# A fused adaLN block: first V as the first matrix work, K and Q weights loaded as halves, softmax denominators as a column of V

## The chip, the core and the metric

The kernel runs on one core of a Trainium2 chip. The metric is the device time of one execution in microseconds (us); lower is better. The core has five engines with a queue each that runs in order: PE (matrix multiply into PSUM, with its weight loads shown as PEld), DVE (vector), ACT (scalar functions, table driven), POOL (general) and SP, which here only issues DMA transfers. They wait for each other through semaphores alone.

## The reference, cut to what matters

S = 2048 tokens, D = 448, H = 16 heads of Dh = 28, F = 1792, all in bf16. Six modulation vectors come from a conditioning row, then follow attention over 8 positions with a stride of 2, and an MLP.

```
mod = silu(c) @ w_mod                      # sa, ca, ga, sb, cb, gb
h = layernorm(x) * (1 + ca) + sa
q, k, v = split(h @ wqkv)                  # 16 heads of 28
# position s attends to s, s-2, ..., s-14
attn = softmax(mask(q . k[s - 2w]) * Dh ** -0.5)
x = x + ga * (sum_w attn * v[s - 2w]) @ wo
h = layernorm(x) * (1 + cb) + sb
x = x + gb * (gelu(layernorm(h) @ w1 + b1) @ w2 + b2)
```

## The kernel before, in words

**Tiles.** Tokens lie as pairs: even and odd tokens are two independent sequences (`NS = 2`) of 1024, so that a stride of 2 becomes a stride of 1. Token tiles `p` = 0 to 7 hold 128 positions of both. A tile goes through layer norm (`front_ln`: statistics L455 and L457 on DVE, the power -0.5 at L466 or L468 on ACT or POOL, normalize L477 on DVE, 64 columns doubled by `tail`, L487 to L491), is transposed, and is scaled and shifted into `hT` (`affine`, L501 on DVE or L503 on ACT). Tiles 0 and 1 are transposed by PE (L534), tiles 2 to 7 by DMA (`zT`, L526).

**D = 448 on 128 rows.** The contraction has three full row tiles and a remainder of 64 rows. The remainder is kept twice, in rows 0 to 63 and 64 to 127, so that two remainder matmuls run side by side (`summed`: L547 full, L553 remainder; L561 is the first, piecewise form of L547).

**Q and K.** For tiles 0 and 1 the weights are first copied into groups of 32 columns per head (`spread`, L438 to L441, and `spread r`, L446 to L449), and Q and K come out transposed (`front_qk`, evacuated at L608). For tiles 2 to 7 (`natural_qk`) the raw weights are the moving operand, ACT or DVE brings the result to SBUF (`zy`, L627, L628), and a DMA transposes it into `qT` or `kT` (L630).

**Attention** runs in 9 batches of 114 positions. V of a batch is 16 matmuls (L705, batches 0 to 4) or 8 matmuls on windows copied by L688 (batches 5 to 8), evacuated into `vb` (L720 on ACT, L723 on DVE). `vb` has 32 columns per head, of which 28 hold V and 4 are zero. Logits `lt` (L737) go through exp on ACT (L744, two halves) and a mask product on DVE (L750). Then PE forms the denominators, `pd` (L759: ones times the masked exponentials, 8 matmuls of 464 columns), and the products `po` (L770, 64 rows in the trace). The denominator is inverted on ACT as exp(-ln): L779 reads `pd` from PSUM, L781 follows. DVE multiplies `po` by it into `qT` (`omul`, L787). After that come the output projection `pw` (L802), the second norm, and the MLP (`p` at L547, L553 and L882, gelu at L863).

**Phases.** Batches 0 to 4 come before the first MLP tile, batches 5 and 6 before the second, 7 and 8 before the last two; between them ACT changes its function table (L924, L931).

**Order.** Nothing is scheduled by rule at run time. `add` records tasks with the engines that could run them, and two tables of numbers, `ORDER` (the sequence in which tasks are recorded, with `:A`, `:D`, `:P`, `:R` for a task put on ACT, DVE, POOL or in its second form on PE, and `+n@m` for n dummy matmuls ahead) and `SLOTS` (the buffer of each short-lived tile), give the order on every queue. PSUM has four such slots (`P`, two banks each), shared by all matmul outputs.

**Loads.** All large loads are issued by SP in one queue: `load_x` L338, modulation weights L345 and L348, `load_qk` L324 (three row tiles of K and Q together), `load_rest` L328 (the 64 remainder rows, twice), `load_wv` L332 and L334. The dummy matmuls (`filler`, L381) multiply zeros.

Of the kernel before, what the change touches and what calls it, by code (L numbers as in the profile page):

```python
# [9 lines left out]
FP32 = mybir.dt.float32  # L10
# [39 lines left out]
]  # L50
ORDER = """
3 14 17 0 1 15 5 9 10 18 11 16 13 19 20 2 6 24 21 73 55+12@55 26 12 71 25 56 72 74 57 75 22 58 77 23 59 62 60 27 61 76
4 32 67 66 78 68+11@68 108 63 28 110 64 30 84:A 89:P 69 79 65 31 70 88:P 109 111 80 83 112:P 34 81 87:A 85 29 93:P
90:A 101+9@101 114 113 36 82 94+3@94 91 95 115:D 92:A 102 86 103 116 144 96 120:A 97 99 135 104 106 117:A 98 142 118:A
105 145 119:A 143 133 146 100 121 136 134 148 137 126 107 147 7 149:D 138 127 150 122 139 124 129 198 190 123 140 191
200 141 199 128 269 125 271 236 270 130 207 40 209 33 201 241 210 38 237 208 272 238 273 37 185 242 152 202 35 154 151
153:A 8 278 187 239 203 159 211 204 188 205:D 212 206 155 279 213 186 243 240 214:A 160 156 192 215 307 157 189 275
161 274 158 280 171 308 281 282 193 162 172 244 245 284 195 283 163 217 173 285 246 276:D 219 39 218 167 216 277 247
447 164 196 248 225 286 168 224 165 169:D 174 312 42 309 313 228 166 310 314 220 170 226 311 290 221 289 229 222 288
315 194 287 230 558 232 197 317 176 560 233 318 175 316 177 223 249 319 234 49 227 320 250 231 251 559 321 235 345 253  # L60
342 346 373:R 254 252 324 46 255 343 322 44 257 48 340 561 323 325 256 41 326 258 374 51 482 54 378 344 375 52 379 299
347 47 259 376 43 328 292 327 300 341 260 348 291 329 301 261 330 295 293 262 263 380 350 264 294 131 296 132 304 333
297 303 377 45 351 334 331 381 265 349 332 305 266 335 382 352 267:A 483 383 268 337 336 384 448 338:D 339 385 353 53
# [3 lines left out]
455 369 434 371 490 372 456 403 443 491 488 435 444 404:D 457 405 458 459 493 492 436 494 460 437 495 461 594 517 438  # L67
462 496 497 463 536 498 499 595 525 500 537 596:D 524 538 539 466 464 501 502 467 465 518 503 528 468 526 527 470 505
529 504 506 531 469 519 507 530 521 471 520 510 472 523 540 522 543 475 508 553 532 541 476 473 533 474 509 542 511
535 562 565 534 477 551 557 512 513 552 563 514 478 515:D 566 479 564 600 480 597 567 554 544 598 481 601 568 445 569  # L70
570 602 547 555 571 599 556 548 572 516 603 604 605 545 606 573 628 607 546 574 608 635 609 549 610 550 636 611 439
575 630 640 576 612 629 637 577 639 613 578 614 638 579 641 581 633 580 634 582 632 583 631 586 647 584 585 587 616
588 615 648 617 642 656 645 618 644 621 649 589 658 622 619 646 620 643 623 650 664 625 590 624 591 651 626:D 592 654
662 653 627 665 655 657 652 663 659 674 660 666 667 669 661 675 668 676 678 677 679 686 672 673 670 687 681 671 690
680 691 688 689 694 693 701 683 692 682 684 695 685 702 697 703 704 709 698 696 710 699 705 711 700 706 712 707 708
# [77 lines left out]
def kernel(  # L153
# [74 lines left out]
    ones_k = cst.tile([128, 2, HP], BF16, name="ones_k")  # L228
# [62 lines left out]
    def consts():  # L291
        for vb in vbufs:
            nc.vector.memset(vb[:, :, :, DH:HP], 0.0)
        nc.vector.memset(ones_k[:], 1.0)
        nc.vector.memset(ones_k[0:WIN - 1, 1, :], 0.0)

    dconst(0.45, consts, ["vpad", "ones"])
# [92 lines left out]
    add("PE", 0.45, c_cols, mode="32x128", reads=["c", "c1", "one1", "warm_w"], bufs=[psc], fills=[psc], name="c_cols")  # L390
    add("ACT", 0.12, lambda: nc.scalar.activation(out=e_c[:], in_=psc.t[:, 0, 0:128 * KT:128], func=ACT.Exp, scale=-1.0), bufs=[psc],
# [117 lines left out]
    def front_ln(u, on_act, dma=False):  # L509
# [452 lines left out]
```

## Time and profile before

| | |
|---|---|
| median of 3 runs | 170.06 us (169.41 to 172.02) |
| the profiled execution | 170.37 us |
| its span in the trace | 168.6 us, so 1.8 us lie around it |
| PE busy | 160.9 us |
| DVE busy | 113.2 us |
| ACT busy | 101.3 us |
| POOL busy | 42.0 us |
| granted TensorE clock | 1.0 |

The rows of the trace name line, engine, operation and tiles (out<-in), a count (x), and times in us or, for one instruction, in ns. A busy time counts an instruction from its start to its end as the profiler sees it. Instructions of one engine overlap a little there, so the pitch from start to start is often shorter than the duration.

### The profile page before, as it was taken

The numbers are of one execution on the slowest core, as the hardware profiler recorded it, in microseconds if no ns is written. First come the engines' busy times: TensorE is split into PE (matmuls) and PEld (weight loads), VectorE is DVE, ScalarE is ACT, GpSimd is POOL, SyncE is SP. The second block draws the span as 40 slices with busy tenths as digits, with TensorE's granted clock in tenths as the row PEclk, the third lists the DMA queues.
The fourth block names the chain that finished last, engine by engine and source line by source line (L and its number), as shares of the span: only waits on it lengthen the run. The fifth ranks groups of instructions, "written<-read, shape, count | busy, mean of one in ns | idle before, by whom it ended". The sixth has DMA issues, their size and how long they took to land.

```text
span 168.6 us, 4965 instructions
## 1 busy us (share of the span) xinstructions
PE 160.9 (95%) x2126; PEld 84.0 (50%) x2126; DVE 113.2 (67%) x277; ACT 101.3 (60%) x139; POOL 42.0 (25%) x69
## 2 busy tenths in 40 slices
PE   7999969987999999999999999999999999999992
PEld 4778535444554544435565443555544455344562
DVE  7869898758899969897837869465596940400112
ACT  3378888949379946869557167986318440099000
POOL 3235251002030400319300033850003156008100
PEclk9999999999999999999999999999999999999999
DMA  5999989699999799300150000028020006110002
GB/s 158 323 336 291 167 253 172 129 158 255 188 227 287 211 160 201 100 0 0 25 106 2 4 0 2 4 49 188 4 95 14 0 4 120 46 67 0 0 27 82
DMA packets 35573, 18.78 MB, mean 111 GB/s; under 512 B 28507, under 2 KB 34592, under 8 KB 35552
## 3 DMA queue, kind: packets, MB, share of 16 engines
q1 hardware_dynamic: 35548, 18.47, 47.6%
q8 instruction: 16, 0.26, 0.6%
q14 instruction: 5, 0.04, 0.1%
q10 hardware_dynamic: 4, 0.00, 0.0%
HBM read 9.81 MB, written 1.84 MB: 69 GB/s over the span
## 4 chain that ended last, share of the span: by engine, by line
PE 77%; DMA 13%; DVE 4%; issue 2%; POOL 2%; SPq 1%; ACT 1%; POOLq 0%; DVEq 0%
PE p L882 26%; PE p L547 22%; PE pw L802 7%; DMA zT<-zy 7%; PE pq L547 5%; PE p L553 4%; DMA x_all<-in_A_x_dram 4%; PE pv L547 3%; PE po L770 3%; DMA wm_st<-in_w_mod_dram 3%; PE lt L737 2%; DVE hT L501 2%; PE pv L705 2%; PE pd L759 1%; DVE stt L455 1%
## 5 line engine op out<-in xcount | busy, mean ns | idle before, releaser
L863 ACT ACTIVATE hm<-p,b_col 128x512 bf16<-128x512 f32 x56 | 33.6, 695 | 30.6 <-PE p L553 26.1
L882 PE MATMUL p<-w_s,hm 128*128 128x448 bf16 (+1 forms) x238 | 44.5, 342 | 0.0
L547 PE MATMUL p<-yT,w_s 128*128 128x512 bf16 x168 | 38.1, 380 | 0.0
L468 POOL TENSOR_TENSOR rs_all<-mvs,neg_half 128x2 f32<-128x2 f32 x23 | 16.4, 719 | 75.1 <-DVE mvs L457 75.1
L882 PEld LDWEIGHTS <-hm 128*128 128x128 bf16 x238 | 22.6, 98 | 18.9 <-issue 0.6
L547 PEld LDWEIGHTS <-w_s 128*128 128x128 bf16 x168 | 15.8, 98 | 21.0 <-issue 3.2
L888 DVE TENSOR_TENSOR x_all<-p,x1p 128x896 bf16<-128x896 f32 (+2 forms) x10 | 8.8, 899 | 23.7 <-PE p L882 23.7
L744 ACT ACTIVATE et<-lt 128x928 bf16<-128x928 f32 x18 | 16.1, 940 | 6.7 <-PE lt L737 6.6
L455 DVE BATCH_NORM_STATS2 stt<-x_all 128x6 f32<-128x448 bf16 x32 | 18.6, 610 | 1.6 <-DMA x_all<-in_A_x_dram 1.4
L547 PE MATMUL pq<-wqk_st,hT 128*128 128x448 bf16 x72 | 15.0, 353 | 1.8 <-DVE hT L501 1.5
L840 POOL TENSOR_TENSOR x1p<-x_all,gbb_bc 128x448 f32<-128x448 bf16 x16 | 16.5, 1060 | 0.0
L787 DVE TENSOR_TENSOR qT<-po,den 128x912 bf16<-128x912 f32 x9 | 10.0, 1106 | 7.1 <-ACT den L781 6.7
L802 PE MATMUL pw<-wo_s,qT 128*128 128x448 bf16 x64 | 13.1, 353 | 0.0
L750 DVE TENSOR_TENSOR et<-et,mask 128x928 bf16<-128x928 bf16 x18 | 11.0, 640 | 2.2 <-ACT et L744 2.1
L627 ACT CAST zy<-pq 128x896 bf16<-128x896 f32 x11 | 9.7, 911 | 2.7 <-issue 2.0
L809 DVE TENSOR_TENSOR x_all<-pw,x_all 128x896 bf16<-128x896 f32 x8 | 8.7, 1088 | 3.9 <-PE pw L802 3.9
L779 ACT ACTIVATE den<-pd 128x928 f32<-128x928 f32 x9 | 8.5, 952 | 4.7 <-PE pd L759 4.7
L818 DVE TENSOR_TENSOR h<-h,mod_bc 128x896 bf16<-128x896 bf16 x16 | 10.4, 655 | 0.2
L547 PEld LDWEIGHTS <-hT 128*128 128x128 bf16 x72 | 6.5, 98 | 8.1 <-DVE hT L501 2.0
L455 DVE BATCH_NORM_STATS2 stt<-h 128x6 f32<-128x448 bf16 x16 | 9.5, 611 | 0.1
L781 ACT ACTIVATE den<-den,den_bias 128x928 f32<-128x928 f32 x9 | 9.4, 1068 | 0.2
L802 PEld LDWEIGHTS <-qT 128*128 128x128 bf16 x64 | 6.0, 98 | 6.0 <-issue 0.4
(114 smaller groups left out, 177.3 us busy)
## 6 DMA issues: line engine op xcount, KB each, us to landing
w_s<-in_B_w_dram SPq DMA_DIRECT2D x7, 224.0 KB, 3.3
out_dram<-x_all SPq DMA_DIRECT2D x7, 224.0 KB, 2.0
x_all<-in_A_x_dram SPq DMA_DIRECT2D x3, 448.0 KB, 6.5
wmod<-in_w_mod_dram SPq DMA_DIRECT2D x3, 448.0 KB
w_s<-in_B_w_dram SPq DMA_DIRECT2D x3, 448.0 KB, 4.8
wqk_st<-in_A_wqkv_dram SPq DMA_DIRECT2D x3, 225.0 KB, 4.3
wm_st<-in_w_mod_dram SPq DMA_DIRECT2D x1, 672.0 KB, 4.6
x_all<-in_A_x_dram SPq DMA_DIRECT2D x2, 224.0 KB
```

The costliest lines, as they stand in the source:

```text
L455: add("DVE", 0.53, lambda: nc.vector.bn_stats(out=stt[:, w, b, 0:6], in_=src()), reads=reads, bufs=bufs, after=early if w == b == 0 else ( ...
L468: ways = {"POOL": (0.55 + 0.17 * n, lambda: nc.gpsimd.tensor_tensor(out=r, in0=v, in1=neg_half[:, 0:n], op=ALU.pow))}
L547: nc.tensor.matmul(out(), lhsT=lhs(kt, slice(0, 128)), rhs=rhs(kt, slice(0, 128)), start=first and kt == 0, stop=not first and kt == KT - 2)
L627: add("ACT", 0.80, lambda to=to, src=src: nc.scalar.copy(out=to(), in_=src()), bufs=[pq, st], reads=["zpad"], writes=[(st, 0)], name="evac ...
L744: exps.append(add("ACT", 0.83, lambda half=half, lt=lt: nc.scalar.activation(out=et.t[:, 2 * half:2 * half + 2].rearrange("p r m c -> p r ...
L750: nc.vector.tensor_tensor(out=ev, in0=ev, in1=mask[:], op=ALU.mult)
L787: nc.vector.tensor_tensor(out=qT[:, :, LEAD + q00:LEAD + q00 + 2 * WQ], in0=po.t[:, :, 0:NS * 4 * WQ].rearrange("p j (m c) -> p m j c", c=WQ),
L802: nc.tensor.matmul(pw.t[:, s, 0:D], lhsT=qT[:, KT * s + ft, LEAD + 128 * p:LEAD + 128 * p + 128], rhs=wo_s[:, ft, :], start=(ft == 0), sto ...
L818: add("DVE", 0.55, lambda vec=vec, op=op: nc.vector.tensor_tensor(out=h2.t[:], in0=h2.t[:], in1=vec.unsqueeze(1).to_broadcast([128, NS, D] ...
L840: add("POOL", 1.0, lambda n=n: nc.gpsimd.tensor_tensor(out=x1p.t[:, n, :], in0=xn(p, n), in1=gbb2_bc[:], op=ALU.add), reads=[f"x{p}", "gbb ...
L863: gelus.append(add("ACT", 0.585, lambda f=f, a=a, p1=p1s[g]: nc.scalar.activation(out=hm.t[:, f].rearrange("p n c -> p (n c)"), in_=p1.t[: ...
L882: nc.tensor.matmul(p2.t[:, n, 0:c1 - c0], lhsT=hm.t[:, f, n, q * 128:(q + 1) * 128], rhs=w2_s[:, f, c0:c1], start=(f == parts[0][0]), stop ...
```

## The change

Four things are changed in the code, and with them the two tables are written anew.

1. **Loads.** A helper, `twin`, makes one transfer that reads the 64 remainder rows twice (a first dimension of two with step 0, or of step D for the modulation weights) into all 128 rows. It takes the place of two transfers at the modulation remainder, the V remainder and the Q and K remainder. The K half of the Q and K weights is one transfer (`load_half(1)`, three row tiles of 452 columns) and the Q half another (`load_half(0)`, 448 columns). On SP's queue the order is now: x of tile 0, modulation, V, x of tile 1, V's remainder, K, x of tiles 2 and 3, Q, then the rest of x.
2. **First V.** V of batch 0 is recorded ahead of the first K and Q work, in its second form (remainder first). K comes ahead of Q.
3. **Denominators.** Column 28 of each head's group in `vb` holds 1, so that row 28 of each group of 32 in `po` is the denominator. `pd`, its 8 matmuls a batch and `ones_k` are gone. DVE spreads row 28 over its group of 32 with a `stream_shuffle` from PSUM into `den` (128x912 fp32), and ACT's logarithm then reads `den` from SBUF. For batch 0 the first 7 rows of the ones are set to 0 before its `po` and back to 1 behind it, two small memsets on DVE.
4. **Small.** The norm of tile 0 takes its power -0.5 in two pieces, and eight empty tasks `fl` hold places at which dummy matmuls could write.

```diff
-    dconst(0.45, consts, ["vpad", "ones"])
+            nc.vector.memset(vb[:, :, :, DH:DH + 1], 1.0)
+            nc.vector.memset(vb[:, :, :, DH + 1:HP], 0.0)
...
+    def load_half(half):
+        c0, c1 = half * D, half * D + D + half * (HP - DH)
+        load(lambda: nc.sync.dma_start(out=wqk_st.t[:, :, c0:c1], in_=rows128(A_wqkv[0:(KT - 1) * 128, c0:c1])), 1.15, [f"wqk{half}"], bufs=[wqk_st])
+        load(lambda: nc.sync.dma_start(out=wqr_st.t[:, c0:c1], in_=twin(A_wqkv, c0, c1 - c0)), 0.4, [f"wr{half}"], bufs=[wqr_st])
+
+    def twin(w, c0, n, step=0):
+        ld = w.ap[0][0]
+        return bass.AP(w.tensor, w.offset + (KT - 1) * 128 * ld + c0, [[step, 2], [ld, KS], [1, n]])
...
-    for kt in range(KT - 1):
-        load_qk(kt)
+    load(lambda: nc.sync.dma_start(out=wm_r.t[:], in_=twin(w_mod, 0, D, D)), 0.4, ["wmr"], bufs=[wm_r])
+    load_wv()
+    load_half(1)
     load_x(1, 2)
-    load_rest(0)
-    load_rest(1)
+    load_half(0)
     load_x(2, 4)
-    load_wv()
...
+        ones = lambda value: nc.vector.memset(vb.t[0:WIN - 1, :, :, DH:DH + 1], value)
+        if i == 0:
+            add("DVE", 0.06, lambda: ones(0.0), reads=["vpad"], bufs=[vb], fills=[vb], name="ones")
...
-        add("PE", 0.25, dmm, reads=[(et, 0), (et, 1), "ones"], bufs=[et, pd], fills=[pd], mode="64x32", instr=16, name=f"pd{i}")
...
+        den = sb("den", [128, 2, 4 * NS, WQ], FP32, "den")
+        add("DVE", 1.0, lambda: nc.vector.stream_shuffle(out=den.t[:].rearrange("p j m c -> p j (m c)"), in_=po.t[:, :, 0:NS * 4 * WQ], mask=[DH] * HP),
+            bufs=[po, den], fills=[den], name="spread_den")
+        add("ACT", 0.87, lambda: nc.scalar.activation(out=den.t[:], in_=den.t[:], func=ACT.Ln, scale=DEN_SCALE),
+            bufs=[den], fills=[den], after=[tbl], name="ln_den")
```

What the new tables do shows on the queues. Three places matter below.

**SP, the first loads** (`Wv` and `Wqk` staging `wqk_st`, `wqr_st` are weights, `x_all` the input). Before:

```order
L348 DMA wm_r<-in_w_mod_dram 64x448 x2
L338 DMA x_all<-in_A_x_dram 128x896
L324 DMA wqk_st<-in_A_wqkv_dram 128x900
L328 DMA wqr_st<-in_A_wqkv_dram 64x900 x2
L324 DMA wqk_st<-in_A_wqkv_dram 128x900 x2
L338 DMA x_all<-in_A_x_dram 128x2x896 x2
L332 DMA Wv<-in_A_wqkv_dram 128x3x448
```

Now:

```order
L345 DMA wm_r<-in_w_mod_dram 128x1x448
L332 DMA Wv<-in_A_wqkv_dram 128x3x448
L336 DMA x_all<-in_A_x_dram 128x896
L333 DMA Wv<-in_A_wqkv_dram 128x1x448
L324 DMA wqk_st<-in_A_wqkv_dram 128x3x452
L325 DMA wqr_st<-in_A_wqkv_dram 128x1x452
L336 DMA x_all<-in_A_x_dram 128x2x896
L324 DMA wqk_st<-in_A_wqkv_dram 128x3x448
L325 DMA wqr_st<-in_A_wqkv_dram 128x1x448
```

V has moved from behind x of tiles 2 to 5 to the place ahead of all Q and K weights; Q's half now stands behind x of tiles 2 and 3.

**ACT, the head**, from the copy of silu (`silu_bc`) to the first evacuation of `pq` (`hT` from `ptr` is the scaled and shifted tile 0, then tile 1). Before:

```order
L397 COPY silu_bc<-silu_bf 128x128
L440 COPY Wqk<-wqk_st 128x512
L503 ACTIVATE hT<-ptr,mod_col 128x2x128
L448 COPY Wqr<-wqr_st 64x256
L440 COPY Wqk<-wqk_st 128x512
L503 ACTIVATE hT<-ptr,mod_col 128x2x128
L448 COPY Wqr<-wqr_st 64x256
L503 ACTIVATE hT<-ptr,mod_col 128x2x128 x4
L608 CAST qT<-pq 128x8x128
```

Now:

```order
L501 ACTIVATE hT<-ptr,mod_col 128x2x128 x2
L438 COPY Wqk<-wqk_st 128x512
L463 ACTIVATE rs_all<-mvs 128x2
L464 ACTIVATE rs_all<-rs_all 128x2
L438 COPY Wqk<-wqk_st 128x512
L719 CAST vb_109<-pv 128x32x28
L438 COPY Wqk<-wqk_st 128x512
L501 ACTIVATE hT<-ptr,mod_col 128x2x128
L446 COPY Wqr<-wqr_st 64x256
L501 ACTIVATE hT<-ptr,mod_col 128x2x128 x2
L607 CAST kT<-pq 128x8x128
```

The third weight copy and `L446` are of Q's half, and the three pieces of `hT` of tile 1 stand behind the first of them. POOL has two such Q copies ahead of the powers of -0.5 of tiles 2 and 3.

**DVE, around the first attention batches.** Before, from the first mask product to the first `omul` (L787):

```order
L750 TENSOR_TENSOR et<-et,mask 128x928 x4
L477 TENSOR_SCALAR zy_99<-x_all,mvs,rs_all 128x448 x2
L455 BN_STATS stt<-x_all 128x6
L457 BN_AGGR mvs<-stt 128x2
L477 TENSOR_SCALAR zy_97<-x_all,mvs,rs_all 128x448 x2
L501 TENSOR_SCALAR hT<-zT,mod_col 128x2x256
L490 COPY zy_99<-zy_99 128x2x64
L501 TENSOR_SCALAR hT<-zT,mod_col 128x2x256 x3
L688 COPY hw<-hT 128x1024
L787 TENSOR_TENSOR qT<-po,den 128x8x114
```

Now, from there to the first `omul` (L783) and two rows behind it:

```order
L752 TENSOR_TENSOR et<-et,mask 128x928 x4
L475 TENSOR_SCALAR zy_99<-x_all,mvs,rs_all 128x448
L773 STREAM_SHUFFLE den<-po 128x912
L455 BN_AGGR mvs<-stt 128x2
L773 STREAM_SHUFFLE den<-po 128x912
L475 TENSOR_SCALAR zy_99<-x_all,mvs,rs_all 128x448
L455 BN_AGGR mvs<-stt 128x2
L499 TENSOR_SCALAR hT<-zT,mod_col 128x2x256 x2
L722 CAST vb_110<-pv 128x32x28
L783 TENSOR_TENSOR qT<-po,den 128x8x114
L499 TENSOR_SCALAR hT<-zT,mod_col 128x2x256
L724 MEMSET vb_109 7x32
```

Two shuffles and an evacuation of V now stand between the masks and the first `omul`; a window copy (`hw`) has left this stretch.

Over the whole program DVE gets 9 shuffles, one more evacuation of V and two copies of `Wqr`, and loses 4 `hT` pieces, 3 window copies, 3 copies of `Wqk` and 5 doublings of columns; ACT gets 4 `hT` pieces and 2 window copies, POOL a window copy, 2 copies of `Wqk` and 5 doublings. The dummy matmuls stand as 9, 14, 7 (ahead of the first V) and 2 at the very end, where there were 12, 11, 9 and 3.

More of the change, by code (lines that the diff above doesn't have):

```diff
@@ L56 @@
[L56 to L60, printed above, removed]
@@ L69 @@
[L69 to L73, printed above, removed]
@@ L390 @@
     add("PE", 0.45, c_cols, mode="32x128", reads=["c", "c1", "one1", "warm_w"], bufs=[psc], fills=[psc], name="c_cols")
+    for i in range(8):
+        idle = psum("idle")
+        add("PE", 0.0, lambda: None, reads=["warm_w"], bufs=[idle], fills=[idle], instr=0, name=f"fl{i}")
     add("ACT", 0.12, lambda: nc.scalar.activation(out=e_c[:], in_=psc.t[:, 0, 0:128 * KT:128], func=ACT.Exp, scale=-1.0), bufs=[psc],
@@ L445, in spread @@
             src = lambda rows=rows, c0=c0: heads(wqr_st.t[rows, c0:c0 + D // 2], H // 2)
-            add("DVE", 0.22, lambda rows=rows, src=src: nc.vector.tensor_copy(out=Wqr[rows, half], in_=src()), reads=[f"wr{a}"],
+            add("DVE", 0.22, lambda rows=rows, src=src: nc.vector.tensor_copy(out=Wqr[rows, half], in_=src()), reads=[f"wr{half}"] + ["wr1"] * (1 - half) * a,
                 bufs=[wqr_st], writes=[f"Wr{half}{a}"], port=True, name="spread r",
@@ L715, in v_first @@
                 vmm(range(KT - 1), False)
-            add("PE", 7 * 0.1895 + 0.1, None, reads=["pads", "wv", "wvr0", "wvr1"] + [f"h{kt}_{p}" for kt in range(KT) for p in ps_], bufs=[pv, vb],
+            add("PE", 7 * 0.1895 + 0.1, None, reads=["pads", "wv", "wvr"] + [f"h{kt}_{p}" for kt in range(KT) for p in ps_], bufs=[pv, vb],
                 fills=[pv], instr=32, name=f"v{i}",
```

80 lines of the change are left out of this document (34 added, 46 removed), and 19 rows, old and new, of tables (ORDER, SLOTS).

## The prediction

> **What bounds the kernel now.** The page comes first: its span, its busy times and the summary of the chain of work that ended last.
>
> ```profile
> span 168.6 us, 4965 instructions
> PE 160.9 (95%) x2126; PEld 84.0 (50%) x2126; DVE 113.2 (67%) x277; ACT 101.3 (60%) x139; POOL 42.0 (25%) x69
> PE 77%; DMA 13%; DVE 4%; issue 2%; POOL 2%; SPq 1%; ACT 1%; POOLq 0%; DVEq 0%
> ```
>
> Three quarters of the chain are PE's. Whether that holds everywhere is read from busy times by stage; the columns are PE, PEld, DVE, ACT and POOL, then granted clock, DMA share and GB/s.
>
> ```profile
> 9.20:23.00 13.80, 12.23 (x238) 8.43 (x237) 11.43 (x36) 11.66 (x18) 5.96 (x14) 1.00 0.98 262
> 23.00:39.00 16.00, 14.36 (x232) 7.05 (x233) 12.17 (x30) 12.04 (x16) 1.44 (x3) 1.00 0.99 180
> 39.00:64.80 25.80, 25.67 (x539) 13.33 (x540) 23.27 (x50) 19.32 (x25) 4.29 (x5) 1.00 0.99 215
> 64.80:165.70 100.90, 100.84 (x1047) 49.53 (x1046) 58.51 (x121) 54.84 (x77) 27.44 (x35) 1.00 0.18 41
> 165.70:168.60 2.90, 0.00 (x0) 0.00 (x0) 0.37 (x1) 0.00 (x0) 0.00 (x0) 1.00 0.36 119
> ```
>
> From 64.8 us, where the first MLP tile starts, PE has no gap in 100.9 us and DVE is busy for 58% of them: there a removed matmul is time gained. Up to 64.8 the transfer engines are 98 to 99% busy and DVE stands at 76 to 90%. The chain in order of time shows what that front waits for, and PE's own waits say how long:
>
> ```profile
> 1.26 4.57 DMA wm_st<-in_w_mod_dram
> 6.33 6.03 DMA x_all<-in_A_x_dram
> 22.97 2.44 PE pq L547 x12
> 25.65 5.22 DMA zT<-zy
> 39.13 0.38 PE pd L759 x6
> 155.01 10.64 PE p L882 x70
> ```
>
> ```profile
> PE pq L547 <- DVE hT L501: 1.5, 1, 1.5
> PE pd L759 <- ACT zy L627: 1.3, 1, 1.3
> ```
>
> So the kernel has two parts. Up to 39 us it runs from x of tiles 2 and 3 (landed at 12.4) through norm, DMA transpose and `hT` to the first natural K and Q at 22.97, then through the next transposes; PE idles only 1.5 and 1.3 us at a time there because the planner fills it. From 39 on it is PE.
>
> **Loads and first V.** The head of the trace (in brackets the idle time ahead of an instruction and what ended it), and the sizes of two loads:
>
> ```profile
> 8.26 1.14 PE L381 MATMUL pq<-warm_w 128*128 128x256 bf16 x9
> 9.23 0.38 PE L561 MATMUL pq<-hT,Wqk 128*128 128x256 bf16 x2
> 8.57 0.57 ACT L503 ACTIVATE hT<-ptr,mod_col 128x256 bf16<-128x256 bf16 x1 [0.49 <-DVE mod_col L424]
> 17.29 1.64 PE L705 MATMUL pv<-Wv,hT 128*64 128x448 bf16 x16
> 10.93 0.61 PE L534 MATMUL ptr<-ident,zy 128*128 128x128 bf16 x8
> 12.23 2.79 PE L547 MATMUL pq<-hT,Wqk 128*128 128x256 bf16 x24
> 15.50 0.44 PE L737 MATMUL lt<-qT,kT 28*64 28x58 bf16 x32
> 7.50 0.61 POOL L441 COPY Wqk<-wqk_st 128x512 bf16<-128x512 bf16 x1 [5.39 <-DMA wqk_st<-in_A_wqkv_dram]
> 14.44 1.47 POOL L468 TENSOR_TENSOR rs_all<-mvs,neg_half 128x2 f32<-128x2 f32 x2 [4.44 <-DVE mvs L457]
> x_all<-in_A_x_dram SPq DMA_DIRECT2D x3, 448.0 KB, 6.5
> wqk_st<-in_A_wqkv_dram SPq DMA_DIRECT2D x3, 225.0 KB, 4.3
> ```
>
> By the shapes on SP's queue, 1684 KB follow the modulation weights (landed at 5.83) up to and including x of tiles 2 and 3 (landed at 12.36): two remainders of 56, x of tile 1 224, Q and K 675 and 225, and 448. That is 258 KB per us. In the new order the bytes up to x of tiles 2 and 3 come to the same 1684, so x lands at 12.4 again. V with its remainder (784 KB after the modulation) is there at 8.9, K at 10.6, but Q, 448 KB behind x, only at 14.1.
>
> V of batch 0 needs all four `hT` pieces of tile 0. ACT now makes its two back to back, 8.57 + 2 x 0.57 = 9.7, so V runs from 9.7 to 11.3. Before, the first useful matmul began at 9.23, piece by piece: the first PE work does not start earlier, and the 9 dummies that it "replaces" (1.14 us from 8.26) ran before `hT` existed. Behind V come K of tile 0 and the transpose of tile 1, 16 x 0.116 (2.79 / 24) + 0.6 = 2.5 us, to 13.8; then Q waits for 14.1 and a copy of 0.6, until 14.7. The rest of the head is Q 1.9, tile 1's K and Q 3.7, V of batch 1 1.6 and four logit groups of 0.4: 14.7 + 8.8 = 23.5. Before, the same work was done when `hT` of tiles 2 and 3 came at 22.97. **The wait this adds:** ACT, POOL and DVE each hold a copy of Q's weights in their queues. Behind POOL's two (14.1 + 2 x 0.61 = 15.3) stand the powers of tiles 2 and 3, which began at 14.44 before. `hT` of these tiles is late by up to 0.9 us. I take **+0.5 us** for the start of the natural part, between +0.9 and, if Q lands with the 675 KB of the old order and frees the queues, -0.6.
>
> **Denominators on PE.** `pd` goes in all nine batches; its group, and its pieces on the chain in the last stage:
>
> ```profile
> L759 PE MATMUL pd<-et,ones_k 64*32 64x464 bf16 x72 | 3.5, 364 | 1.3 <-ACT zy L627 1.3
> 85.48 0.32 PE pd L759 x8
> 87.01 0.24 PE pd L759 x8
> 87.26 2.76 PE p L882 x14
> 91.15 3.03 PE pw L802 x16
> 112.14 0.32 PE pd L759 x8
> 115.76 0.32 PE pd L759 x8
> ```
>
> In the last stage 0.32 + 0.24 + 0.32 + 0.32 = **-1.2 us**, at full value by the stage's PE share. In the front five batches, 5 x 0.35 = 1.7 us of PE work. The column itself costs nothing on PE, since `po` already multiplies 32 columns. The two dummies at the very end run beside the last store in the 2.9 us without PE.
>
> The Trainium skill, page "Perfetto Trace Analysis", section "Identifying the Most-Contended Engine", says that matmul busy share is no good measure and that weight-load busy share should be used; here that is 50%, and by it PE has headroom and the 1.2 us would not come: 169.6 us. The trace speaks against it for the last stage (70 matmuls of one group follow each other in 10.64 us on the chain, no wait between), so I keep the 1.2.
>
> **Denominators on DVE.** The shuffle is in no row. Its nearest rows, and those of what DVE gives up:
>
> ```profile
> L787 DVE TENSOR_TENSOR qT<-po,den 128x912 bf16<-128x912 f32 x9 | 10.0, 1106 | 7.1 <-ACT den L781 6.7 <-PE po L770 0.2
> L723 DVE CAST vb<-pv 128x896 bf16<-128x896 f32 x1 | 1.0, 1049 | 0.0
> L501 DVE TENSOR_SCALAR hT<-zT,mod_col 128x512 bf16<-128x512 bf16 x11 | 4.7, 477 | 2.9 <-DMA zT<-zy 2.9
> L688 DVE COPY hw<-hT 128x1024 bf16<-128x1024 bf16 x4 | 1.7, 427 | 0.1
> L779 ACT ACTIVATE den<-pd 128x928 f32<-128x928 f32 x9 | 8.5, 952 | 4.7 <-PE pd L759 4.7
> L781 ACT ACTIVATE den<-den,den_bias 128x928 f32<-128x928 f32 x9 | 9.4, 1068 | 0.2
> ```
>
> `omul` reads the same 912 fp32 columns of PSUM: 1.1 us. Below, half of it, as no row excludes a faster form; above, two passes, 2.2. I take 1.1, as both PSUM readers of this size stand at 1.05 to 1.1. The Trainium skill, page "VectorE: DVE Perf Modes", section "The perf-mode tier table", gives about 2400 ns for a shuffle of 2048 columns and one speed only: an estimate of 1.07 us for 912, which moves the sum by under 0.2; no run so far shows it.
>
> From 23.0 to 64.8 DVE was busy 12.17 + 23.27 = 35.4 of 41.8 us. It gets 5 x 1.1 and one evacuation of V, 1.05, and gives 4 x 0.48 of `hT`, 3 x 0.43 of windows and some doublings (0.5): +2.9, so 38.3. PE needs 14.36 + 25.67 - 1.7 = 38.3. Two engines with the same 38.3 us, which hand each other work at every batch (masks to `po`, `po` to shuffle, `omul` to `pw`, and with `omul` a PSUM slot), can't lie wholly side by side. Before, PE's 40.0 beside DVE's 35.4 took 41.8, 1.8 above the larger; with no slack on DVE I add 2.3 and get 40.6: **-1.2 us**. So the 1.7 us off PE is in part used up by waits for DVE: later `omul`, later free slots for K and Q.
>
> In the last stage the chain `po`, shuffle, logarithm, exponential, `omul` is longer by the shuffle than the old one from `pd`. For batches 5 and 6, from the end of the second `po`: the final addition in front of the shuffles and then two shuffles, two logarithms, one exponential and `omul`, about 5.5 us to the first `omul`. The cover is V of batch 8 and 18 matmuls of `p`, 26 at 0.2 (2.76 / 14), 5.1. For batches 7 and 8 the cover is 20 matmuls (3.9) and the first `pw` (half of 3.03) against 1.1 + 0.95 + 1.07 + 1.11 = 4.2. I take **+0.2**, up to 0.5.
>
> **Sum.** 170.37 + 0.5 - 1.2 - 1.2 + 0.2 = 168.7 us against the profiled execution, which lies 0.3 above the median of the runs: **168.4 us**.
>
> **Rivals.** *PE sets the front too* (0.30): the two waits of 1.5 and 1.3 shrink as ACT and POOL take `hT`, windows and doublings off DVE, and all of `pd` counts. For it: PE is busy for 40.0 of 41.8 us there. Against it: DVE's 38.3. Then -1.2 - 1.7 - 1.8 = -4.7: 165.4 us.
> *Loads slow down* (0.17): halves have rows of 900 bytes, not 1800. At 200 instead of 258 KB per us x of tiles 2 and 3 lands at 14.3, the natural part starts 1.9 later: 170.4 - 1.2 + 0.2 - 1.2 + 1.9 - 0.3 = 169.8 us. For it: DMA is full to 64.8 us. Against it: bytes are equal.
> *DVE overflows* (0.09): the shuffle takes two passes, 2.2 us. DVE's front is 43.8 us, above the stage's 41.8; with 1.2 of waits the stage takes 45, +3.2. In the last stage the two chains lengthen by 2.2 and outrun their covers by 2.6 and 1.0: 170.4 + 0.5 + 3.2 - 1.2 + 3.6 - 0.3 = 176.2 us. It decides from about 1.7 us a shuffle, where DVE fills the 41.8. Against it: the two rows at 1.05 to 1.1.
> That V is not first in effect is part of the forecast: the first useful work starts at 9.7, not before 9.23.
>
> **Numbers.** Forecast 0.44, rivals 0.30, 0.17, 0.09. A measurement of this kernel tells about 2% (3.4 us) from no change, so faster means under 166.7: the first rival and a little of the forecast, 0.34. Slower means above 173.5: the last rival and a rest, 0.10. Within: 0.56. The range, 164.6 to 171.6, holds the forecast, the loads and most of the first rival.
>
> **What would show it.** Right: a shuffle at 1.05 to 1.15 us; first V at 9.5 to 10; Q's copies on ACT and POOL starting at 13.5 or later; the first natural K or Q at 23 to 24; DVE above 90% between 23 and the start of the MLP, that start at 63.5 to 65, and PE gapless behind it. Wrong: MLP starting before 62.5 (PE set the front), after 66 (loads or DVE), or gaps of over 0.5 us before `pw` in the last stage.

## The result, and the profile after

| | before | after |
|---|---|---|
| median of the runs | 170.38 us (169.41 to 172.02, 4 runs) | 178.61 us (178.27 to 179.22, 4 runs) |
| ratio, 95% interval | | 1.0507 (1.0445 to 1.0568): slower |
| profiled execution, its span | 170.37, 168.6 us | 179.22, 177.5 us |

The forecast was 168.4 us with a range to 171.6, so it missed by 10 us, on the other side. In this and later comparisons the ratio leaves out executions in which the chip was in a slower state, so it can differ a little from the quotient of two medians.

The page of the changed kernel:

```profile
span 177.5 us, 4851 instructions
...
PE 163.1 (92%) x2051; PEld 83.7 (47%) x2051; DVE 125.7 (71%) x287; ACT 106.1 (60%) x147; POOL 47.4 (27%) x75
...
PE 79%; DMA 7%; SPq 6%; DVE 2%; ACT 2%; issue 1%; POOL 0%; POOLq 0%; DVEq 0%; ACTq 0%
```

SP's queue (SPq) has 6% of the chain, where it had 1%. The chain in order of time shows where, and when the first natural K or Q starts (22.97 before):

```profile
4.27 3.84 SPq L324
...
9.09 2.42 SPq L336
11.56 7.25 DMA wqk_st<-in_A_wqkv_dram
...
31.94 2.38 PE pq L546 x12
...
74.35 1.46 PE p L546 x6
...
163.77 10.64 PE p L878 x70
```

The last group starts 8.76 us later than before (155.01), and 8.97 of that are there at the first natural matmul. The two later stages, with the columns of the prediction's table of stages (the natural part up to the MLP, the MLP up to the last matmul):

```profile
31.94:74.35 42.41, 39.48 (x728) 19.35 (x728) 38.59 (x79) 36.74 (x43) 7.78 (x11) 1.00 1.03 188
74.35:174.41 100.06, 100.06 (x1018) 49.33 (x1018) 66.34 (x126) 55.07 (x78) 30.45 (x36) 1.00 0.21 47
```

For before the same cuts are:

```profile
22.97:64.84 41.87, 40.10 (x771) 20.45 (x773) 35.52 (x79) 31.44 (x39) 5.75 (x8) 1.00 0.99 202
64.84:165.65 100.81, 100.80 (x1047) 49.49 (x1046) 58.45 (x120) 54.80 (x77) 27.44 (x35) 1.00 0.18 41
```

So the natural part lost 0.5, the MLP won 0.75, and the rest is the head. SP's issues there (start, how long SP was held by the issue):

```profile
1.72 0.70 SPq L345 DMA_DIRECT2D wm_r<-in_w_mod_dram  x1
2.47 0.43 SPq L332 DMA_DIRECT2D Wv<-in_A_wqkv_dram  x1
2.94 0.48 SPq L336 DMA_DIRECT2D x_all<-in_A_x_dram  x1
3.46 0.76 SPq L333 DMA_DIRECT2D Wv<-in_A_wqkv_dram  x1
4.27 3.84 SPq L324 DMA_DIRECT2D wqk_st<-in_A_wqkv_dram  x1
8.15 0.90 SPq L325 DMA_DIRECT2D wqr_st<-in_A_wqkv_dram  x1
9.09 2.42 SPq L336 DMA_DIRECT2D x_all<-in_A_x_dram  x1
11.56 0.93 SPq L324 DMA_DIRECT2D wqk_st<-in_A_wqkv_dram  x1
13.45 3.63 SPq L336 DMA_DIRECT2D x_all<-in_A_x_dram  x2
```

In the kernel before, most of these issues took 0.4 to 0.6 us. Here the remainder transfers (L345, L333, L325) go out in 0.70 to 0.90 us, and the plain loads behind them are held for 3.84, 2.42 and 3.63 us (the last figure is for two loads). What waits for them, from the timeline (in brackets the idle time ahead of the instruction and what ended it):

```profile
13.20 1.78 PE L704 MATMUL pv<-Wv,hT 64*64 64x448 bf16 x16 [0.50 <-DMA Wv<-in_A_wqkv_dram]
...
16.70 0.22 DVE L444 COPY Wqr<-wqr_st 64x256 bf16<-64x256 bf16 x1 [3.85 <-DMA wqr_st<-in_A_wqkv_dram]
...
18.88 0.62 ACT L438 COPY Wqk<-wqk_st 128x512 bf16<-128x512 bf16 x1 [6.84 <-DMA wqk_st<-in_A_wqkv_dram]
...
19.56 0.82 PE L560 MATMUL pq<-hT,Wqk 128*128 128x256 bf16 x3 [4.58 <-ACT Wqk L438]
```

V, forecast for 9.7, runs at 13.20; K's weights, forecast to land at 10.6, are copied from 18.88 on, and PE waits 4.58 us for the first copy. The shuffle is not the matter:

```profile
L773 DVE STREAM_SHUFFLE den<-po 128x912 f32<-128x912 f32 x9 | 10.5, 1179 | 0.0
```

### The profile page after: what moved, and what is told of

Read it like the earlier page. It is cut to its first block, busy times and chain, and to the rows that moved or that the text cites. A ratio compares the mean times of both kernels' runs of the same rounds, so it can differ in the third digit from the quotient of the medians.

```text
span 177.5 us, 4851 instructions
## 1 busy us (share of the span) xinstructions
PE 163.1 (92%) x2051; PEld 83.7 (47%) x2051; DVE 125.7 (71%) x287; ACT 106.1 (60%) x147; POOL 47.4 (27%) x75
## 4 chain that ended last, share of the span: by engine, by line
PE 79%; DMA 7%; SPq 6%; DVE 2%; ACT 2%; issue 1%; POOL 0%; POOLq 0%; DVEq 0%; ACTq 0%
PE p L878 24%; PE p L546 21%; PE pq L546 9%; PE pw L798 5%; DMA wqk_st<-in_A_wqkv_dram 4%; PE p L552 4%; PE po L764 3%; PE lt L739 3%; DMA yT<-zy 3%; PE pv L704 3%; SPq L324 2%; PE pq L552 2%; SPq L336 2%; PE pv L546 1%; PE pq L560 1%
## 5 line engine op out<-in xcount | busy, mean ns | idle before, releaser
L859 ACT ACTIVATE hm<-p,b_col 128x512 bf16<-128x512 f32 x56 | 34.2, 690 | 30.9 <-PE p L552 25.3
L546 PE MATMUL p<-yT,w_s 128*128 128x512 bf16 x168 | 38.3, 379 | 1.5 <-DMA yT<-zy 1.5
L466 POOL TENSOR_TENSOR rs_all<-mvs,neg_half 128x2 f32<-128x2 f32 x22 | 17.9, 813 | 53.6 <-DVE mvs L455 53.6
L836 POOL TENSOR_TENSOR x1p<-x_all,gbb_bc 128x448 f32<-128x448 bf16 x16 | 17.8, 1128 | 0.0
L775 ACT ACTIVATE den<-den 128x912 f32<-128x912 f32 x9 | 8.6, 961 | 7.7 <-DVE den L773 7.6
L814 DVE TENSOR_TENSOR h<-h,mod_bc 128x896 bf16<-128x896 bf16 x16 | 12.2, 763 | 0.4
L475 DVE TENSOR_SCALAR zy<-h,mvs,rs_all 128x448 bf16<-128x448 bf16 x16 | 8.4, 566 | 4.8 <-POOL rs_all L466 4.8
L783 DVE TENSOR_TENSOR qT<-po,den 128x912 bf16<-128x912 f32 x9 | 9.8, 1103 | 2.3 <-ACT den L777 2.2
L773 DVE STREAM_SHUFFLE den<-po 128x912 f32<-128x912 f32 x9 | 10.5, 1179 | 0.0
L704 PE MATMUL pv<-Wv,hT 128*64 128x448 bf16 (+1 forms) x80 | 8.7, 368 | 0.9 <-DMA Wv<-in_A_wqkv_dram 0.5
```

What stands on the lines that cost most here:

```text
L466: ways = {"POOL": (0.55 + 0.17 * n, lambda: nc.gpsimd.tensor_tensor(out=r, in0=v, in1=neg_half[:, 0:n], op=ALU.pow))}
L546: nc.tensor.matmul(out(), lhsT=lhs(kt, slice(0, 128)), rhs=rhs(kt, slice(0, 128)), start=first and kt == 0, stop=not first and kt == KT - 2)
L704: nc.tensor.matmul(pv.t[WK * j:WK * j + WK, s, 0:D], lhsT=hT[rows, NS * kt + s, kc + j * WQ:kc + j * WQ + WK], rhs=Wv[rows, kt, :], start= ...
L814: add("DVE", 0.55, lambda vec=vec, op=op: nc.vector.tensor_tensor(out=h2.t[:], in0=h2.t[:], in1=vec.unsqueeze(1).to_broadcast([128, NS, D] ...
L836: add("POOL", 1.0, lambda n=n: nc.gpsimd.tensor_tensor(out=x1p.t[:, n, :], in0=xn(p, n), in1=gbb2_bc[:], op=ALU.add), reads=[f"x{p}", "gbb ...
L859: gelus.append(add("ACT", 0.585, lambda f=f, a=a, p1=p1s[g]: nc.scalar.activation(out=hm.t[:, f].rearrange("p n c -> p (n c)"), in_=p1.t[: ...
```

## Experiments

**Theories.** *1:* the one-transfer remainders are the loss. Their source has an outermost dimension of 2, only a few of the 16 DMA engines carry them, and all plain loads have to share those engines' queues (the expectations below call them rings). The Trainium skill, page "DMA: Bandwidth & Descriptors", section "Rules for kernel authors", states it: "an outermost dim of size c < 16 — e.g. a leading zero-stride broadcast of c copies — confines the whole DMA to at most c engines". The prediction missed this rule. *2:* the halves of K and Q, with rows of 900 bytes, are slow. *3:* the new order of loads is late by itself. *4:* the shuffles and the chain behind `po` cost more than `pd` did. Theory 5 came out of the first runs.

**Pairs in place of one transfer.** Each remainder again by two transfers of 64 rows, at the same places of the queue (here for Q and K; V and the modulation likewise).

```diff
+    def two(dst, w, c0, n, step=0):
+        for a in range(2):
+            nc.sync.dma_start(out=dst(slice(KS * a, KS * a + KS)), in_=w[(KT - 1) * 128:D, c0 + step * a:c0 + step * a + n])
...
-        load(lambda: nc.sync.dma_start(out=wqr_st.t[:, c0:c1], in_=twin(A_wqkv, c0, c1 - c0)), 0.4, [f"wr{half}"], bufs=[wqr_st])
+        load(lambda: two(lambda r: wqr_st.t[r, c0:c1], A_wqkv, c0, c1 - c0), 0.4, [f"wr{half}"], bufs=[wqr_st])
```

> The changed kernel with every remainder loaded by two transfers of 64 rows, as before the change, in the same places of the queue; all else as changed. Theory 1 (a source whose outermost dimension is 2 is carried by two of the 16 DMA engines, which holds up all loads behind it): the first natural K or Q goes back from 31.9 to about 23.5 us, the time to 170.5 us (168.5 to 172). Theory 2 (the halves of K and Q, with their rows of 900 bytes, are slow) and theory 3 (the new order of the loads is late by itself): the first natural matmul stays at 30 to 32 us, the time at 177 to 179.

Measured: 173.50 us (172.5 to 174.8, 4 runs), ratio 1.0193 (1.0123 to 1.0263). Against the changed kernel's 1.0507 the pairs win 3.1%, 5.3 us; theory 1 has most of the loss, but 2% is left. Its chain:

```profile
8.63 4.59 DMA wqk_st<-in_A_wqkv_dram
...
13.97 1.46 PE pq L564 x6
...
25.89 2.38 PE pq L550 x12
```

SP's issue of K's half is back from 3.84 to 0.59 us:

```profile
5.29 0.59 SPq L328 DMA_DIRECT2D wqk_st<-in_A_wqkv_dram  x1
```

The first natural matmul is back by 6.05 us, not by 8.4. K's first copy still starts only at 13.30:

```profile
13.30 0.62 ACT L442 COPY Wqk<-wqk_st 128x512 bf16<-128x512 bf16 x1 [3.25 <-DMA wqk_st<-in_A_wqkv_dram]
```

**One-transfer remainders alone, in the kernel before.** Here for Q and K; the modulation and V likewise.

```diff
-        load(lambda a=a: nc.sync.dma_start(out=wqr_st.t[KS * a:KS * a + KS, :], in_=A_wqkv[(KT - 1) * 128:D, 0:2 * D + HP - DH]),
+        load(lambda a=a: None if a else nc.sync.dma_start(out=wqr_st.t[:], in_=twin(A_wqkv, 0, 2 * D + HP - DH)),
```

> The kernel before with one edit: the remainder rows of the modulation weights, of K and Q and of V come by one transfer each, as in the change; order of loads, whole K and Q rows, order of work and denominators as before. Theory 1: 337 KB ahead of x of tiles 2 and 3 ride on two rings, against 449 KB in the changed kernel, so the first natural matmul moves from 22.97 to about 29.5 us and the time to 176.5 us (174 to 179). Theories 2 and 3: no change, 170 us.

Measured: 178.32 us (176.72 to 178.83, 4 runs), ratio 1.048 (1.0407 to 1.0554). This one edit costs as much as the whole change; theories 2 to 4 are in none of it. The chain:

```profile
3.42 11.44 DMA wqr_st<-in_A_wqkv_dram
...
29.41 2.38 PE pq L550 x12
```

225 KB took 11.44 us from issue to landing, 20 KB per us, where a plain load of 225 KB had taken 4.3 us in the kernel before and the prediction had read 258 KB per us for all loads together. As an estimate, two of 16 engines would have 32 of the 258, and they carry their share of the plain loads as well. The profile gives only a mean over the 16 engines, but it speaks for two. Below is the stretch from 11 to 12 us, first in the changed kernel, where SP is held by the issue of a plain load until 11.51, then with pairs. The mean share of the engines (the last figure but one) is 0.14 in the one, which is 2.2 of 16, and 1.08 in the other:

```profile
11.00:12.00 1.00, 1.00 (x7) 0.75 (x6) 1.00 (x5) 0.97 (x2) 0.00 (x0) 0.50 0.14 48
```

```profile
11.00:12.00 1.00, 0.59 (x8) 0.11 (x2) 0.28 (x2) 0.00 (x0) 0.00 (x0) 1.00 1.08 369
```

**Outermost dimension 2 or 16, same rows and bytes.** The pairs again, with the 64 rows of each walked as 2 x 32 (the source below) or, with 16 in place of 2, as 16 x 4.

```diff
+            src = bass.AP(w.tensor, w.offset + (KT - 1) * 128 * ld + c0 + step * a, [[ld, 2], [2 * ld, KS // 2], [1, n]])
+            nc.sync.dma_start(out=dst(slice(KS * a, KS * a + KS)), in_=src)
```

> As the kernel with two transfers of 64 rows for each remainder, but the source of each walks its 64 rows as 2 x 32, the odd ones after the even ones, so that its outermost dimension is 2 and no row is read twice; the remainder rows of the weights come to lie in another order, so the output is not the reference's. Theory 1: the same bytes on the same two engines as in the changed kernel, in eight transfers and not four: 178.5 us (176 to 181). If what is slow is the reading of the same rows twice by one transfer (a step of 0), 170.5 us.

> As the kernel before in this list, with the 64 rows walked as 16 x 4: outermost dimension 16, the same number of transfers, rows and bytes, the rows again in another order. Theory 1: all 16 engines carry each transfer, 170.5 us (168.5 to 172), as with plain rows. If it is the broken order of the rows that costs, as slow as with 2 x 32.

Measured: 177.99 us (177.66, 178.31) with 2 and 173.83 us (173.20, 174.46) with 16. The first natural matmul of the one and the other:

```profile
31.31 2.44 PE L552 MATMUL pq<-wqk_st,hT 128*128 128x448 bf16 x12
```

```profile
26.44 2.44 PE L552 MATMUL pq<-wqk_st,hT 128*128 128x448 bf16 x12 [0.73 <-DVE hT L505]
```

With 2 the loss is that of the changed kernel though no row is read twice; with 16 it is that of plain pairs. So neither the repeated rows nor the broken row order costs, and the outermost size decides. (The 170.5 expected for 16 was missed for the reason next found.)

**Modulation's remainder alone by one transfer.**

```diff
-    load(lambda: two(lambda r: wm_r.t[r, :], w_mod, 0, D, D), 0.4, ["wmr"], bufs=[wm_r])
+    load(lambda: nc.sync.dma_start(out=wm_r.t[:], in_=twin(w_mod, 0, D, D)), 0.4, ["wmr"], bufs=[wm_r])
```

> The changed kernel with the remainders of V, K and Q by two transfers each, so that only the modulation's remainder (112 KB, its two copies from different columns, the first in the queue) still comes by one transfer with an outermost dimension of 2. Theory 1: the two rings carry 112 KB more, at 16 KB per us each 3.5 us, part of which passes while other rings are filled behind: between the 173.5 us with no such transfer and the 178.6 with four, 175 us (174 to 177). If only the copies that read one row twice are slow, 173.5 us.

Measured: 174.77 and 179.16 us. Two runs so far apart give no size; only the sign (not below 173.5) fits theory 1.

**K and Q in tiles of their own.** Theory 5: the wait that the program sets ahead of a copy out of `wqk_st` takes in the load of Q's half, since both halves lie in one tile. The edit is made to the kernel with pairs, for the loads, the copies and the natural K and Q; the lines show its form.

```diff
+    wk_st = cst.tile([128, KT - 1, D + HP - DH], BF16, name="wk_st")
+    st_of = lambda half: wk_st if half else wqk_st.t
...
-            dst, src = (lambda k0=k0, n=n: Wqk[:, k0:k0 + n, half]), (lambda k0=k0, n=n: heads(wqk_st.t[:, k0:k0 + n, half * D:half * D + D], H))
+            dst, src = (lambda k0=k0, n=n: Wqk[:, k0:k0 + n, half]), (lambda k0=k0, n=n: heads(st_of(half)[:, k0:k0 + n, 0:D], H))
```

> The changed kernel with two transfers of 64 rows per remainder, and with K's half and K's remainder in tiles of their own instead of one tile with Q's. What is left of the loss there (173.5 us against 169.9) has two explanations. Theory 5: with both halves in one tile the copies of K's weights wait for Q's half too, which was queued 3.3 us behind (K's first copy began at 13.30, with Q's landing at 13.22). Then K's copies begin at 10 to 11 us, the first natural matmul comes at 23.5 to 24.5 instead of 25.8, and the time is 171 us (169.5 to 172). Theory 2 (K's half, with 384 rows of 900 bytes, itself lands late): K's copies begin at 13 as before, 173.5 us.

Measured: 170.95 us (168.78 to 173.39, 10 runs) beside 169.66 for before, ratio 1.0025 (0.9976 to 1.0075): no loss that can be told. Theory 5 holds. Timeline, then the same two stages:

```profile
9.13 1.64 PE L713 MATMUL pv<-Wv,hT 64*64 64x448 bf16 x16
...
9.75 0.62 ACT L447 COPY Wqk<-wk_st 128x512 bf16<-128x512 bf16 x1 [0.37 <-DMA wk_st<-in_A_wqkv_dram]
...
13.28 1.15 DVE L462 BATCH_NORM_STATS2 stt<-x_all 128x6 f32<-128x448 bf16 x2 [1.83 <-DMA x_all<-in_A_x_dram]
...
14.38 0.62 ACT L447 COPY Wqk<-wqk_st 128x512 bf16<-128x512 bf16 x1 [2.36 <-DMA wqk_st<-in_A_wqkv_dram]
```

```profile
24.40:66.05 41.65, 39.60 (x727) 19.25 (x728) 38.39 (x82) 36.87 (x44) 7.62 (x11) 1.00 1.05 197
66.05:166.11 100.06, 100.06 (x1018) 49.34 (x1018) 67.40 (x127) 55.03 (x78) 29.81 (x36) 1.00 0.22 47
```

V starts at 9.13 and K's copies at 9.75: without the one-transfer remainders and the false wait the prediction's times (9.7 and 10.6) come out, a little early, and Q's copies start at 14.38, where the prediction had Q land at 14.1.

The shared tile alone does not make this wait. In the kernel before, three loads fill `wqk_st`, each one row tile, and the first copy starts at 7.50 (the prediction's row of POOL), though the third load was issued only at 5.9 and such a load took 4.3 us to land. The two halves differ from these in that each writes some columns of all three row tiles.

**Whole rows of Q and K, in K's place.** Again from the kernel with pairs, one tile.

```diff
-        load(lambda: nc.sync.dma_start(out=wqk_st.t[:, :, c0:c1], in_=rows128(A_wqkv[0:(KT - 1) * 128, c0:c1])), 1.15, [f"wqk{half}"], bufs=[wqk_st])
+        load(lambda: [nc.sync.dma_start(out=wqk_st.t[:, kt, :], in_=A_wqkv[kt * 128:kt * 128 + 128, 0:2 * D + HP - DH]) for kt in range(half * (KT - 1))],
+             1.15, [f"wqk{half}"], bufs=[wqk_st])
```

> The changed kernel with two transfers of 64 rows per remainder, and with Q and K loaded as whole rows of 1800 bytes, one transfer per 128 rows, all three and the remainder in K's place; nothing in Q's place. Theory 5 (K waits for the last of the two halves whatever their rows): K's first copy, which then needs only its own 128 rows, begins at 9.5 to 10.5 us, 171 us (169.5 to 172.5). Theory 2: the same, from faster transfers; the kernel with tiles of their own tells the two apart. Theory 3 (V first is itself a late order): 173.5 us or more, with the first natural matmul at 25.5 or later.

Measured: 171.77 us, ratio 1.0116 (1.0069 to 1.0162). K's first copy:

```profile
9.12 0.61 POOL L444 COPY Wqk<-wqk_st 128x512 bf16<-128x512 bf16 x1 [5.64 <-DMA wqk_st<-in_A_wqkv_dram]
```

Both versions end the wait (9.12 here, 9.75 with tiles of their own), and that with rows of 900 bytes is no slower (ratio 1.0025), so theory 2 falls: rows of 900 bytes cost no time that can be seen here. Theory 3's 173.5 did not come either.

**One-transfer remainders with tiles of their own.** The edit of the tiles, with `twin` left at all four remainders.

```diff
+        load(lambda: nc.sync.dma_start(out=str_of(half)[:, 0:n], in_=twin(A_wqkv, c0, n)), 0.4, [f"wr{half}"], bufs=[wqr_st])
```

> The changed kernel with K and Q in tiles of their own, and its four remainder transfers left as they are, each with an outermost dimension of 2. If the two losses add up (5.1 us for the two rings, 2.5 for the common tile): 178.6 - 2.5 = 176 us (175 to 177). If the late loads on two rings hide the common tile, 178.5; if K's wait for Q's half, which stood behind those transfers, was most of the loss, 173 or below.

Measured: 177.74 and 178.47 us. The two losses don't add: with the remainders on few engines, the tiles of their own win only 0.5 us by the medians (0.9 by the ratios, 1.0457 against 1.0507). Timeline, then chain:

```profile
14.61 0.62 ACT L447 COPY Wqk<-wk_st 128x512 bf16<-128x512 bf16 x1 [2.22 <-DMA wk_st<-in_A_wqkv_dram]
...
19.32 0.62 ACT L447 COPY Wqk<-wqk_st 128x512 bf16<-128x512 bf16 x1 [1.95 <-DMA wqk_st<-in_A_wqkv_dram]
```

```profile
12.80 10.06 DMA wqr_st<-in_A_wqkv_dram
```

K is copied 4.3 us earlier than in the changed kernel, but then the head waits for Q's remainder, 113 KB that take 10.06 us and land at 22.86. So the one-transfer remainders cost 5.3 us beside the common tile and about 7 (4.3%) without it; the common tile costs 2.9 (1.7%) where the loads are quick.

**Without the shuffles.** From the kernel with tiles of their own; ACT reads `po` itself, with an exponential in place of the logarithm.

```diff
-        add("DVE", 1.0, lambda: nc.vector.stream_shuffle(out=den.t[:].rearrange("p j m c -> p j (m c)"), in_=po.t[:, :, 0:NS * 4 * WQ], mask=[DH] * HP),
+        add("DVE", 1.0, lambda: None,
...
-        add("ACT", 0.87, lambda: nc.scalar.activation(out=den.t[:], in_=den.t[:], func=ACT.Ln, scale=DEN_SCALE),
+        add("ACT", 0.87, lambda: nc.scalar.activation(out=den.t[:].rearrange("p j m c -> p j (m c)"), in_=po.t[:, :, 0:NS * 4 * WQ], func=ACT.Exp, scale=1e-6),
```

> The kernel with two transfers of 64 rows per remainder and K and Q in tiles of their own (170.95 us), with its nine shuffles left out: ACT reads po itself where it read the spread denominators, with an exponential of the same 912 columns for the logarithm, so the output is not the reference's. This prices what the shuffles cost in the planned order. By the prediction's ledger (DVE as full as PE in the front, small losses behind po): 9 x 1.18 us less on DVE bring 0.5 to 1.5 us, 170 us (169.3 to 170.6). Theory 4 (the shuffles and their chain cost more than pd cost on PE): 2.5 us or more, 168.5 or below.

Measured: 170.58 us, ratio 0.9972 (0.9923 to 1.0021), against 1.0025 (0.9976 to 1.0075) for the same kernel with shuffles: 0.5% or 0.9 us, but the intervals overlap, so no gain is shown. Theory 4, which asked for 2.5 us, falls. Its two stages:

```profile
22.81:64.01 41.20, 39.26 (x727) 19.50 (x728) 33.45 (x72) 36.42 (x44) 7.38 (x11) 1.00 1.05 196
64.01:164.85 100.84, 100.22 (x1018) 49.47 (x1018) 63.61 (x119) 54.73 (x78) 29.75 (x36) 1.00 0.21 48
```

DVE is relieved of 4.9 us in the natural part, and the stage is only 0.45 shorter. The MLP is 0.78 longer (100.84 against 100.06), so the two stages together win nothing; this execution is shorter than that with shuffles only because its head ended at 22.81 and not at 24.40.

**The column in the kernel before.** No `pd`; `column` issues the shuffle and the logarithm right behind the matmuls of `po`.

```diff
-        add("PE", 0.25, dmm, reads=[(et, 0), (et, 1), "ones"], bufs=[et, pd], fills=[pd], mode="64x32", instr=16, name=f"pd{i}")
-        lt_mms.append(add("PE", 0.55, pmm, reads=[(et, 0), (et, 1)], bufs=[et, vb, po], fills=[po], mode="64x32", instr=128,
+        add("PE", 0.25, lambda: None, reads=[(et, 0), (et, 1), "ones"], bufs=[et, pd], fills=[pd], mode="64x32", instr=16, name=f"pd{i}")
+        lt_mms.append(add("PE", 0.55, lambda: (pmm(), column()), reads=[(et, 0), (et, 1)], bufs=[et, vb, po], fills=[po], mode="64x32", instr=128,
```

> The kernel before with the denominators alone changed: the column of ones in V, the shuffle on DVE right behind po's matmuls, then the logarithm, and no pd matmuls; loads, their order and the order of the work as before. For batches 0, 2 and 3 the exponential moves behind po with them. By the terms of the prediction (1.2 less in the last stage, 1.2 less in the front, 0.2 more behind po): 168.2 us (167 to 169.5). Theory 4 (the shuffles cost more on DVE and behind po than pd cost on PE): 170 us or more.

Measured: 182.41 us, ratio 1.074 (1.0659 to 1.0822). This is far from 168.2 us. It lies above theory 4's 170, but it does not bear on that theory, because it prices something else: the old order starts the logarithm from `pd`, ahead of `po`, and now ACT stands still until the shuffle is done, with the rest of its queue behind it. From its waits (total, times, longest):

```profile
ACT den L788 <- DVE den L787: 15.9, 7, 4.4
...
DVE qT L799 <- ACT den L782: 8.8, 6, 2.2
```

So in the old order the column loses 12.6 us; its price in an order that suits it is not to be had from this run.

**x of tiles 2 and 3 ahead of K.** Only the place of that load in the order, first with K and Q in tiles of their own, then with whole rows. In the order of tasks (22 and 23 are K's half and its remainder, 27 is x):

```diff
-22 79 61 11 76 23 62 63 27
+27 22 79 61 11 76 23 62 63
```

> The kernel with two transfers of 64 rows per remainder and K and Q in tiles of their own, with x of tiles 2 and 3 queued ahead of K's half and not behind it. There x landed at 13.28 us (12.36 before the change) and the first natural matmul came at 24.4 (22.97 before). The 451 KB of K, at some 310 KB per us, are 1.45 us: x at 11.8, the first natural matmul at 23.0, K's first copy at 11.2 and not 9.75, and 169.5 us (168.3 to 171). If K, 1.45 later, is what the head waits for instead, 171 us or more.

> The kernel with two transfers of 64 rows per remainder and with whole rows of Q and K (171.77 us), with x of tiles 2 and 3 queued ahead of Q and K. There x landed at 12.72 us behind 900 KB of Q and K. Ahead of them it lands at about 10, Q and K at 12.5 to 13. If the head runs from x: the first natural matmul 1.4 us earlier or more and 170.3 us; if Q and K are late instead, 172 us or more.

Measured: 171.39 us, ratio 1.0102 (1.0067 to 1.0137), and 173.38 us, ratio 1.0157 (1.0092 to 1.0223). Neither helps; in the first K becomes what the head waits for:

```profile
11.34 0.62 ACT L447 COPY Wqk<-wk_st 128x512 bf16<-128x512 bf16 x1 [1.96 <-DMA wk_st<-in_A_wqkv_dram]
...
12.02 0.61 PE L569 MATMUL pq<-hT,Wqk 128*128 128x256 bf16 x4 [1.25 <-ACT Wqk L447]
```

None of the versions beats the kernel before.

**PE kept busy through the wait.** In the changed kernel PE idles from 15.0 to 19.6 us, and the granted clock is 0.97 from 16 to 17 us and 0.50 from 17 to 23. Dummy matmuls behind the first V, in the kernel with pairs (22) and in the changed kernel (42), keep it up. Entry 107 of the order is K's first matmul:

```diff
-107
+107+22@107
```

> The kernel with two transfers of 64 rows per remainder (173.5 us; K and Q in one tile), with 22 dummy matmuls of 256 columns put on PE behind the first V, in the 2.4 us in which it waits for K's copies. Without them the granted clock there falls to 0.50 from 14 to 17 us. If the slow clock is part of the loss: PE keeps 1.00, the work of these 3 us is done 1.5 us earlier, 172 us (171 to 172.8). If only the late weights count: 173.5 us.

> The changed kernel with 42 dummy matmuls of 256 columns on PE behind the first V, in the 4.6 us in which it waits for K's copies. Without them the granted clock is 0.50 from 17 to 23.5 us. If the slow clock is part of the loss: 1.00 there, and what follows is done up to 2 us earlier, 176.5 us (175.5 to 177.8). If only the late weights count: 178.6 us.

Measured: 173.76 us, ratio 1.0218 (1.0159 to 1.0276), and 178.32 us, ratio 1.0484 (1.0413 to 1.0554): both as without dummies. One microsecond of the changed kernel without and with them (the column behind POOL is the granted clock):

```profile
21.00:22.00 1.00, 1.00 (x10) 0.59 (x10) 1.00 (x4) 0.67 (x2) 1.00 (x3) 0.50 0.59 186
```

```profile
21.00:22.00 1.00, 1.00 (x10) 0.51 (x8) 0.94 (x3) 1.00 (x4) 0.71 (x1) 1.00 0.14 48
```

With the dummies the clock is 1.00, and the time is the same within 0.3 us. The slow clock accompanies the loss and is no part of it that can be measured.

## Why the prediction was wrong, point by point

- **Loads and first V: this step failed.** It set every byte at 258 KB per us ("the bytes up to x of tiles 2 and 3 come to the same 1684, so x lands at 12.4 again"). That took it for granted that a transfer's bytes spread over all engines whatever its shape. The four remainder transfers do not (225 KB in 11.44 us in the kernel before with them, and a mean share of 0.14 in the changed one), and the loads queued behind are held up. Forecast for the start of the natural part +0.5 (between -0.6 and +0.9); measured +8.97. The price 5.3 us is shown by the pairs, and its cause by the sizes 2 and 16.
- **K at 10.6 had a second hole.** Only the half's own landing was counted. In one tile with Q, K's copies wait for both: 2.9 us where the loads are quick, mostly hidden by the first loss in the changed kernel itself. With both taken away V and K come at 9.13 and 9.75, and the wait for Q that the prediction did count is there (14.38).
- **The rival "Loads slow down"** had the right place. Its mechanism, rows of 900 bytes, was wrong (whole rows are no faster), and its 1.9 us were a fifth of the delay. The signs given for it were right: an MLP that starts after 66 (74.35 here) meant loads or DVE.
- **Denominators on PE: -2.9 us of PE work were too much** (1.2 in the last stage, 1.7 in the front). From before to the kernel with tiles of their own PE's busy time falls by 0.74 in the MLP and by 0.5 in the natural part. So the summed durations of the groups, 1.2 us in the last stage, were more than their removal took from PE there. By the weight-load rule of the Trainium skill (page "Perfetto Trace Analysis", section "Identifying the Most-Contended Engine"), as the prediction read it and set it aside, none of the last stage's 1.2 would have come; 0.75 did.
- **Denominators on DVE: the occupancy was right, its price not.** DVE was to have 38.3 us in the natural part and had 38.59 (38.39 with tiles of their own). But the 1.2 us to be won there did not come (41.65 against 41.87). DVE is not what withheld them, since 4.9 us less of it brings 0.45; PE itself needs 39.6 where 38.3 was forecast. What holds the other 2 us there was not tried.
- **Last stage:** -1.2 + 0.2 forecast, -0.75 measured. PE had no gap there (100.06 of 100.06 us), so the 0.2 of waiting did not come, and the -1.2 was too large. The shuffle took 1.18 us, where 1.05 to 1.15 was to show the step right. "DVE overflows" was not the case (by the prediction's own terms it decides from 1.8 us a shuffle rather than 1.7), and "PE sets the front too" neither.
- **Sum without the two faults:** +1.43 (natural part from 22.97 to 24.40), -0.22 and -0.75 make +0.46 us, against the forecast of -1.7. That kernel is measured as the same as before. Its +1.43 lies above the forecast's +0.9, and the 0.93 beyond +0.5 is about what x of tiles 2 and 3 was late (13.28, not 12.36); why it was late is open, and in another execution it was not (last section).

## What to carry to other kernels

Before merging two transfers into one, look at the outermost dimension of the source: here a 2 there cost 5.3 us, where the issue that it saved takes SP some 0.5 us (1.20 for the two at the modulation's remainder, 0.70 for the one), and the price was paid by the loads queued behind as well. When a load is split into column halves that are used at different times, split the tile that it lands in too, or the first half may wait for the last. A step moved out of a planned order, such as the column without its plan, says nothing about the price of that step.

## What the runs showed of the hardware

- SP's own issue is held behind transfers with an outermost dimension of 2: 3.84 us for a load that takes 0.59 with pairs. In the changed kernel the plain loads pay, and the narrow ones go out in 0.7 to 0.9. With eight narrow transfers (2 x 32) some of those are held too: the two of K's remainder take SP 2.61 us, and 1.11 as plain pairs.
- A granted clock of 0.50 over several microseconds of the head cost less than the runs can tell (173.50 us with it and 173.76 without, 178.61 and 178.32).
- With the same loads the head varies from execution to execution: x of tiles 2 and 3 landed at 13.28 us in the profiled run with tiles of their own, and was there at 11.57 in the one without shuffles, with first natural matmuls at 24.40 and 22.81. Why is open.
